# Float32 score matmuls in place of three float32r passes in the second attention step

## The chip, the core and the metric

The kernel runs on one core of one Trainium2 chip. TensorE (PE in the profile, with its weight loads as PEld) multiplies matrices, VectorE (DVE) and ScalarE (ACT) work element by element, GpSimd (POOL) does a few element-wise operations beside them, and SyncE (SP) issues most of the DMAs. The metric is the device time of one execution in microseconds (us), the median of several runs.

## What is computed

The reference is a two-step attention followed by two feed-forward layers:

```python
def sm_attn(qq, kk, vv):
    s = scale * np.matmul(qq, kk.transpose(0, 1, 3, 2))
    s = s - np.max(s, axis=-1, keepdims=True)
    a = np.exp(s)
    a = a / (np.sum(a, axis=-1, keepdims=True) + 1e-09)
    return np.matmul(a, vv)
p_packed = sm_attn(p, k, v)            # 32 packs attend to 576 tokens
out = sm_attn(q, p_packed, p_packed)   # 576 tokens attend to 32 packs
...
x = out.transpose(0, 2, 1, 3).reshape(4608, 512)
h = x @ w_in;  x = (h * np.cos(h)) @ w_out                 # first layer, d_ff 2048
h = x @ w_in2; x = (P(h) / (Q(h) + 1e-6)) @ w_out2         # second layer, d_ff 2048
```

There are 8 batches of 8 heads, 576 tokens, a head dimension of 64 and 32 packs. All values are float32. The change is in the scores of the second `sm_attn`: queries against packed rows.

## The kernel before, in words

The work is cut into groups of one batch and four heads, 16 groups in all (two per batch, `g` = 0 and 1). Most matmuls run on float32r operands: a float32 value `x` is carried as `hi + lo`, and a product takes the three passes of `PASSES` (hi·hi, hi·lo, lo·hi). `split` (lines 65 to 67) makes such a pair: ACT copies the value into `hi` (L66) and another engine subtracts to get `lo` (L67).

The kernel has four stretches.

1. *Pack attention* (to about 204 us in the profile). For each group `prep` transposes k on DVE into `kT` (L177) and lays p out block-diagonally on POOL (`pbd`, L182). `s1` takes the scores of packs against tokens with float32 operands (four matmuls, L209), then come the softmax (L217 to L228), the transposes `et` (L238), the product with v (`pv`, L249), and `wunit` (L283), which multiplies the packed rows with the first layer's input weights. Beside this, `conv_w1i` turns these weights from float64 words into float32r pairs: `convert` (lines 74 to 93) is four instructions on DVE (L82, L87, L89, L90), three on ACT (L80, L88, L92) and two on POOL (L91, L93) for each 128x512 block.
2. *Conversion of the first layer's output weights* (`conv_w1o`, some 204 to 281 us), in which the first slots of the next stretch already run.
3. *First layer* (about 281 to 930 us). There are 128 slots, each with 12 matmuls for `h` (`mm_h`, L530), an element-wise chain on ACT and DVE (`chain1`, L554 to L561, then `finish_g`, which splits `g` into `gh` and `gl`), and 24 matmuls for `y` two slots later (`mm_y`, L574). `h` has two PSUM buffers: PE can start the `h` of a slot only when the last DVE instruction that reads the one before last (L561) is done. `split_wq` (four blocks for each batch, ACT L66 and POOL L67) and `conv_w2` (one block in three slots) run beside it.
4. *Second layer* (from 930 us), with no POOL work at all.

The second attention step is `attn2_steps`, a generator that is advanced between other work: for batch 0 inside stretch 1, for batches 1 to 7 inside stretches 2 and 3, one step every second slot. For one group it loads q and the packed rows, transposes both on DVE (`qT` L327, `ppT` L333), and **splits both**: ACT writes `qh` and `pph`, POOL subtracts to get `ql` and `ppl`, through L66 and L67. One step later come twelve float32r matmuls (`scores`, L193) into a PSUM buffer that it shares with `h` (tag "h") or, in stretch 1, with `s1`. DVE transposes the scores out (`sT`, L343) and the softmax follows.

The instructions of an engine run in the order in which they stand in its queue. That order is set by a scheduler that works on the program as a whole; `hold` keeps some instructions behind a given matmul. In stretch 1 `qT` shares its two buffers with `kT`, and `ppT` with `pbd` (the table `tg0`).

## Time and profile before

| what | value |
|---|---|
| runs | 1743.73, 1744.01, 1751.22 us; median 1744.01 us |
| span of the profiled execution | 1744.9 us |
| PE busy | 1619.0 us, 93% of the span |
| DVE busy | 1424.5 us, 82% |
| ACT busy | 1175.8 us, 67% |
| POOL busy | 355.0 us, 20% |
| mean granted TensorE clock | 0.973 of full |

Busy time of an engine is the time in which at least one of its instructions ran. A matmul's record is longer than the distance to the next one, since matmuls are pipelined; the distance between starts tells what a matmul costs in a stream. A float32 matmul of the program shows as two records. The span differs from the median of the runs by 0.9 us; no other time of the profiled execution is listed.

### The profile page before, as it was taken

Reading aid. Unit: us, or ns where it says so; the run is one execution under the profiler, and the core shown is the slowest. Engines: PE = TensorE matmul, PEld = TensorE weight load, DVE = VectorE, ACT = ScalarE, POOL = GpSimd, SP = SyncE. Lnnn points to the kernel's source line nnn. Section 1 sums busy time; section 2 is a strip of 40 time slices with the busy share of each in tenths; the row PEclk is TensorE's granted clock in tenths of the full one; section 3 lists DMA queues with packets and bytes.
Section 4 is the critical chain, followed back from the end, with each engine's and each line's share of the span. In section 5 each row is a group of like instructions: output and inputs, shape, how many; then the busy total and the mean of one; then the engine's idle time right before and its main releaser. Section 6 shows DMA issues by size and latency. Waiting matters only on the chain.

```text
span 1744.9 us, 24418 instructions
## 1 busy us (share of the span) xinstructions
PE 1619.0 (93%) x8896; PEld 1419.4 (81%) x8896; DVE 1424.5 (82%) x2143; ACT 1175.8 (67%) x1917; POOL 355.0 (20%) x235
## 2 busy tenths in 40 slices
PE   5889578999899989899999999999999999999996
PEld 3668378989899989889898888888888888888884
DVE  6993598798889889988867888888888888888884
ACT  4554566666656566666547787878787878787874
POOL 4650553434334434343300000000000000000000
PEclk9989789999999999999999999999999999999998
DMA  9897822443434434433348020202020202020000
GB/s 291 249 258 234 271 88 83 135 134 113 141 120 134 135 122 136 140 129 107 130 161 304 1 72 1 72 1 73 1 73 1 73 0 72 2 72 1 31 19 25
DMA packets 99768, 183.52 MB, mean 105 GB/s; under 512 B 11584, under 2 KB 46400, under 8 KB 99648
## 3 DMA queue, kind: packets, MB, share of 16 engines
q1 hardware_dynamic: 92224, 163.09, 29.3%
q10 hardware_dynamic: 7424, 18.88, 3.5%
q8 instruction: 70, 1.15, 0.3%
q14 instruction: 50, 0.41, 0.1%
HBM read 117.97 MB, written 63.96 MB: 104 GB/s over the span
## 4 chain that ended last, share of the span: by engine, by line
PE 66%; DVE 20%; ACT 5%; issue 4%; DMA 3%; POOL 1%; SPq 0%; ACTq 0%; DVEq 0%
PE h L659 23%; PE o L718 23%; PE y L574 11%; PE h L530 6%; DVE gl L67 3%; DVE u L555 3%; DVE cvp L89 2%; DVE r L556 2%; DVE cvp L87 2%; DVE g L561 2%; DVE cvf L90 1%; DVE cvf L82 1%; DMA st<-in_moe_w_in_dram 1%; PE w L283 1%; PE s L209 1%
## 5 line engine op out<-in xcount | busy, mean ns | idle before, releaser
L574 PE MATMUL y<-gh,w1o 128*128 128x288 f32 x2048 | 431.8, 297 | 2.3 <-DVE yl L67 2.3
L659 PE MATMUL h<-x,w 128*128 128x512 f32 x1728 | 422.7, 393 | 0.0
L659 PEld LDWEIGHTS h<-x,w 128*128 128x128 f32 x1728 | 324.1, 188 | 74.2
L574 PEld LDWEIGHTS y<-gh,w1o 128*128 128x128 f32 x2048 | 338.1, 190 | 3.8 <-DVE yl L67 3.2
L718 PE MATMUL o<-w,g2h 128*128 128x512 f32 x1152 | 334.0, 394 | 1.3 <-ACT g2h L677 1.3
L574 PE MATMUL y<-gl,w1o 128*128 128x288 f32 x1024 | 298.7, 297 | 15.0 <-DVE gl L67 14.7
L530 PE MATMUL h<-ah,wq 128*128 128x288 f32 x1024 | 236.2, 307 | 46.0 <-DVE g L561 43.2
L718 PEld LDWEIGHTS o<-w,g2h 128*128 128x128 f32 x1152 | 216.0, 188 | 53.1 <-ACT g2h L677 2.1
L530 PEld LDWEIGHTS h<-ah,wq 128*128 128x128 f32 x1024 | 179.5, 197 | 51.0 <-issue 49.4
L574 PEld LDWEIGHTS y<-gl,w1o 128*128 128x128 f32 x1024 | 193.3, 189 | 18.9 <-DVE gl L67 18.9
L718 PE MATMUL o<-w,g2l 128*128 128x512 f32 x576 | 199.9, 393 | 0.0
L693 ACT ACTIVATE sq<-h 128x512 f32<-128x512 f32 x144 | 87.4, 607 | 155.7 <-PE h L659 155.6
L560 ACT ACTIVATE r<-r,coef 128x576 f32<-128x576 f32 x128 | 99.1, 775 | 103.1 <-DVE r L556 102.4
L695 DVE SCALAR_TENSOR_TENSOR ab<-sq,coef,ab 128x512 f32<-128x512 f32 x144 | 108.1, 751 | 67.8 <-ACT ab L694 67.5
L530 PE MATMUL h<-al,wq 128*128 128x288 f32 x512 | 156.1, 305 | 0.0
L67 DVE TENSOR_TENSOR gl<-g,gh 128x576 fp32r<-128x576 f32 x128 | 126.3, 989 | 18.0 <-ACT gh L66 16.3
L704 DVE SCALAR_TENSOR_TENSOR ab<-ab,y 128x512 f32<-128x512 f32 x144 | 99.5, 691 | 48.1 <-ACT y L701 47.5
L91 POOL TENSOR_TENSOR cvf<-cvf,cvs 128x512 f32<-128x512 f32 x64 | 88.2, 1377 | 217.7 <-DVE cvf L90 216.5
L554 ACT ACTIVATE u<-h,coef 128x576 f32<-128x576 f32 x128 | 93.8, 734 | 54.3 <-PE h L530 53.8
L718 PEld LDWEIGHTS o<-w,g2l 128*128 128x128 f32 x576 | 108.0, 188 | 25.6
L696 ACT ACTIVATE c<-h,coef 128x512 f32<-128x512 f32 x144 | 114.1, 792 | 9.8 <-DVE g2l L683 9.8
L561 DVE TENSOR_TENSOR g<-h,r 128x576 f32<-128x576 f32 x128 | 95.9, 750 | 30.1 <-ACT r L560 29.9
(97 smaller groups left out, 2775.6 us busy)
## 6 DMA issues: line engine op xcount, KB each, us to landing
x<-yd SPq DMA_DIRECT2D x36, 512.0 KB
w<-w2d SPq DMA_DIRECT2D x68, 256.0 KB
st<-in_moe_w_in_dram SPq DMA_DIRECT2D x32, 512.0 KB
wd<-wev ACTq DMA_DIRECT2D x64, 256.0 KB
st<-in_moe_w_out_dram SPq DMA_DIRECT2D x32, 512.0 KB
wq<-wd SPq DMA_DIRECT2D x32, 512.0 KB
kx<-in_k_dram SPq DMA_DIRECT2D x16, 576.0 KB
vx<-in_v_dram SPq DMA_DIRECT2D x48, 192.0 KB
```

What stands on the lines that cost most here:

```text
L67: lo_eng.tensor_tensor(out=lo, in0=src, in1=hi.bitcast(F32), op=ALU.subtract)
L91: nc.gpsimd.tensor_tensor(out=ff, in0=ff, in1=sg, op=ALU.mult)
L530: last_h[0] = nc.tensor.matmul(out=ps[:, u, 0:HS], lhsT=wq[:, g, a, o:o + 128], rhs=a_t[b, g][c][:, hf * HS:hf * HS + HS], start=(i == 0), ...
L554: nc.scalar.activation(out=u, in_=ph, func=AF.Identity, scale=INV2PI, bias=coef[:, 6:7])
L560: nc.scalar.activation(out=r, in_=r, func=AF.Sin, bias=coef[:, 7:8])
L561: nc.vector.tensor_tensor(out=gt, in0=ph, in1=r, op=ALU.mult)
L574: nc.tensor.matmul(out=y_t[d][:, 0:HS], lhsT=w1o_s[f // 4][a][:, f % 4, 128 * d:128 * d + 128], rhs=gs[c][:, u], start=(f == 0 and i == 0) ...
L659: nc.tensor.matmul(out=ps, lhsT=w2_s[f][:, 0, a, 128 * kk:128 * kk + 128], rhs=x_t[t, c, kk], start=(i == 0), stop=(i == 3 * NKD - 1),)
L695: nc.vector.scalar_tensor_tensor(out=ab, in0=sq, scalar=coef[:, 5:6], in1=ab, op0=ALU.mult, op1=ALU.add)
L696: nc.scalar.activation(out=c1, in_=ph, func=AF.Identity, scale=coef[:, 3:4], bias=coef[:, 2:3])
L704: nc.vector.scalar_tensor_tensor(out=ab, in0=ab, scalar=QC, in1=y0, op0=ALU.add, op1=ALU.mult)
L718: nc.tensor.matmul(out=o_t[s], lhsT=g2_t[n][a][:, 128 * s:128 * s + 128], rhs=w2_s[f][:, 1, c], start=(f == 0 and i == 0), stop=(f == NFC ...
```

## The change

`scores` now takes one float32 operand on each side and makes four matmuls for a group (two halves of the tokens, two blocks of the head dimension) where it made twelve. `s1`, which had the same loop written out, calls it. In `attn2_steps` both splits are gone, with their four tiles and with their instructions on ACT and POOL; the matmuls read `qT` and `ppT` themselves.

```diff
-        def scores(ps, lhs, rhs, lhs_of):
-            for hf in range(2):
-                i = 0
-                for e in range(NDB):
-                    for a, c in PASSES:
-                        nc.tensor.matmul(
-                            out=ps[:, hf, 0:HS],
-                            lhsT=lhs_of(lhs[a], e),
-                            rhs=rhs[c][:, e, hf * HS:hf * HS + HS],
-                            start=(i == 0),
-                            stop=(i == 3 * NDB - 1),
-                        )
-                        i += 1
...
+        def scores(ps, lhs, rhs):
             for hf in range(2):
                 for e in range(NDB):
                     nc.tensor.matmul(
                         out=ps[:, hf, 0:HS],
-                        lhsT=pbd[:, e],
-                        rhs=kT[:, e, hf * HS:hf * HS + HS],
+                        lhsT=lhs[:, e],
+                        rhs=rhs[:, e, hf * HS:hf * HS + HS],
                         start=(e == 0),
                         stop=(e == NDB - 1),
                     )
...
-                qs = [tile([128, NDB, S], F32R, nm) for nm in ("qh", "ql")]
-                split(*qs, qT.rearrange("p e c j -> p e (c j)"), nc.gpsimd)
-                ps = [tile([128, NDB, 4 * M], F32R, nm) for nm in ("pph", "ppl")]
-                split(*ps, ppT.rearrange("p e h m -> p e (h m)"), nc.gpsimd)
...
-                scores(sc, ps, qs, lambda x, e: x[:, e])
+                scores(sc, ppT.rearrange("p e h m -> p e (h m)"), qT.rearrange("p e c j -> p e (c j)"))
```

Line numbers after the change are smaller by 12 from L217 to L333 and by 16 from L343 on; `s1`'s matmuls, L209 before, are L191 now, and so are those of the second step.

On POOL, in the conversion of the first layer's output weights (`cvf` and `w1o` are its blocks), the difference between the two orders is this:

```order
 L93 TENSOR_TENSOR w1o<-cvf,w1o 128x512
 L91 TENSOR_TENSOR cvf<-cvf,cvs 128x512
-L67 TENSOR_TENSOR ql<-qT,qh 128x1152
-L67 TENSOR_TENSOR ppl<-ppT,pph 128x256
 L93 TENSOR_TENSOR w1o<-cvf,w1o 128x512
 L91 TENSOR_TENSOR cvf<-cvf,cvs 128x512
```

The two subtractions are gone and their neighbours stand as they stood. The same holds for the other 15 pairs but for a few neighbours that change places.

On DVE, in the middle of the first layer (the step of batch 4 that begins with `qT`; `cvf` and `cvp` belong to a block of `conv_w2`, `yl` to the split of `y`, `gl`, `u`, `r` to the element-wise chain), the rows before are:

```order
L82 TENSOR_SCALAR cvf<-st_5045 128x512
L327 STREAM_TRANSPOSE qT<-qx 128x18x2x32
L333 STREAM_TRANSPOSE ppT<-ppx 128x4x2x32
L87 TENSOR_SCALAR cvp<-cvf 128x512
L67 TENSOR_TENSOR yl<-y_4569,yh 128x288
L67 TENSOR_TENSOR gl<-g,gh 128x576
L555 TENSOR_SCALAR u<-u 128x576
L67 TENSOR_TENSOR yl<-y_4570,yh 128x288
L89 TENSOR_TENSOR cvp<-st_5045,cvp 128x512
```

and now:

```order
L82 TENSOR_SCALAR cvf<-st_4917 128x512
L315 STREAM_TRANSPOSE qT<-qx 128x18x2x32
L321 STREAM_TRANSPOSE ppT<-ppx 128x4x2x32
L87 TENSOR_SCALAR cvp<-cvf 128x512
L67 TENSOR_TENSOR yl<-y_4441,yh 128x288
L67 TENSOR_TENSOR gl<-g,gh 128x576
L539 TENSOR_SCALAR u<-u 128x576
L67 TENSOR_TENSOR yl<-y_4442,yh 128x288
L89 TENSOR_TENSOR cvp<-st_4917,cvp 128x512
```

Nothing moved at this place on DVE.

On DVE, in the pack attention, around the first scores of batch 0 (`kT` is the next groups' k for `s1`, `sT` takes the scores out of PSUM; in brackets the engines and DMA queues waited for), the rows before are:

```order
L177 STREAM_TRANSPOSE kT<-kx 128x3x6x32 [waits DMAHW2_49,Pool_49]
L177 STREAM_TRANSPOSE kT<-kx 128x3x6x32
L67 TENSOR_TENSOR wl_328<-pt,wl_327 128x64 [waits Activation_49]
L217 TENSOR_REDUCE mx<-s_545 128x1 [waits PE_49]
L177 STREAM_TRANSPOSE kT<-kx 128x3x6x32 [waits DMAHW2_49]
L177 STREAM_TRANSPOSE kT<-kx 128x3x6x32
L82 TENSOR_SCALAR cvf<-st_311 128x512 [waits DMAHW3_49,Pool_49]
```

and now, where the second pair is further down:

```order
L205 TENSOR_REDUCE mx<-s_537 128x1 [waits PE_49]
L177 STREAM_TRANSPOSE kT<-kx 128x3x6x32 [waits DMAHW2_49]
L177 STREAM_TRANSPOSE kT<-kx 128x3x6x32
L87 TENSOR_SCALAR cvp<-cvf 128x512 [waits DVE_49]
...
L67 TENSOR_TENSOR wl_328<-pt,wl_327 128x64 [waits Activation_49]
L327 STREAM_TRANSPOSE sT<-s_629 128x576 [waits PE_49]
L177 STREAM_TRANSPOSE kT<-kx 128x3x6x32 x2
L90 SCALAR_TENSOR_TENSOR cvf<-cvp,cvf 128x512 [waits DVE_49,Activation_49]
```

A pair of k's transposes that took over the buffer of `qT` waited for POOL's subtraction; it now stands behind the transpose of the scores, since the buffer is free only when the score matmuls have read it.

## Rows read from the trace of the kernel before

**Rows 1.** Stretches: us, busy us of each engine (instructions), granted clock, DMA share, GB/s

```profile
36.00:123.00 87.00, 67.97 (x289) 52.42 (x287) 84.18 (x142) 47.63 (x95) 51.70 (x40) 0.86 0.90 253
204.00:281.00 77.00, 52.15 (x340) 50.36 (x340) 71.38 (x91) 45.07 (x71) 42.14 (x29) 0.84 0.35 111
281.00:930.00 649.00, 610.34 (x4444) 601.05 (x4445) 548.08 (x773) 398.87 (x600) 224.30 (x129) 0.98 0.41 134
930.00:1744.90 814.90, 798.75 (x3455) 647.04 (x3453) 662.62 (x1012) 630.06 (x1047) 0.00 (x0) 0.99 0.13 42
```

**Rows 2.** Groups of instructions: count, busy us, mean ns, idle before

```profile
L67 POOL TENSOR_TENSOR ql<-qT,qh 128x1152 fp32r<-128x1152 f32 x16 | 44.3, 2771 | 41.6 <-ACT qh L66 41.6
L66 ACT ACTIVATE qh<-qT 128x1152 fp32r<-128x1152 f32 x16 | 18.7, 1168 | 10.0 <-DVE qT L327 10.0
```

**Rows 3.** Timeline from 499.8 us: start, us, instruction, idle before it

```profile
500.02 2.98 POOL L67 TENSOR_TENSOR ql<-qT,qh 128x1152 fp32r<-128x1152 f32 x1 [7.42 <-ACT qh L66]
500.73 2.81 DVE L89 TENSOR_TENSOR cvp<-st,cvp 128x512 f32<-128x512 uint32 x1
...
506.65 0.58 PE L530 MATMUL h<-ah,wq 128*128 128x288 f32 x1 [2.40 <-DVE g L561]
```

**Rows 4.** DVE instructions by tile: duration ns, min/median/max

```profile
L555 DVE TENSOR_SCALAR u<-u x128: 396/454/2918, 215.3 to 919.9; 128x576 f32<-128x576 f32 x128
L87 DVE TENSOR_SCALAR cvp<-cvf x64: 382/427/2627, 16.4 to 836.4; 128x512 uint32<-128x512 uint32 x64
L89 DVE TENSOR_TENSOR cvp<-st,cvp x64: 643/692/2902, 17.6 to 840.6; 128x512 f32<-128x512 uint32 x64
L90 DVE SCALAR_TENSOR_TENSOR cvf<-cvp,cvf x64: 641/682/3111, 19.3 to 841.6; 128x512 f32<-128x512 f32 x64
```

**Rows 5.** Chain that ended last: start, us, what

```profile
43.03 2.37 DVE cvp L87
...
67.73 3.03 DVE cvf L90
...
231.97 2.84 DVE u L555
```

**Rows 6.** Timeline from 259.5 us, DVE

```profile
260.35 3.09 DVE L90 SCALAR_TENSOR_TENSOR cvf<-cvp,cvf 128x512 f32<-128x512 f32 x1
```

**Rows 7.** Twelve stretches of 8 us, each from a start of `ql` after 281

```profile
500.00:508.00 8.00, 5.60 (x39) 5.40 (x38) 7.83 (x11) 4.30 (x8) 5.58 (x4) 0.89 0.59 206
...
615.40:623.40 8.00, 4.84 (x26) 4.64 (x25) 7.25 (x11) 4.65 (x9) 3.54 (x2) 0.72 0.41 152
...
769.80:777.80 8.00, 5.59 (x38) 5.38 (x38) 7.83 (x11) 4.29 (x8) 5.58 (x4) 0.88 0.58 200
...
sum 96.00, PE 82.89 PEld 80.72 DVE 90.39 ACT 57.48 POOL 53.29; mean PE 6.91 PEld 6.73 DVE 7.53 ACT 4.79 POOL 4.44
```

**Rows 8.** Float32 matmuls of `s1`, by tile: duration ns, min/median/max

```profile
L209 PE MATMUL s<-kT,pbd x128: 403/406/847, 9.0 to 159.1; 128*128 128x288 f32 x128
```

**Rows 9.** Chain, the same matmuls of two groups

```profile
107.13 3.62 PE s L209 x8
...
133.05 1.94 PE s L209 x8
```

**Rows 10.** Timeline of PE: first score matmul of a group, first matmul behind it

```profile
248.01 0.29 PE L193 MATMUL s<-qh,pph 128*128 128x288 f32 x1
...
249.60 0.30 PE L574 MATMUL y<-gh,w1o 128*128 128x288 f32 x1
```

**Rows 11.** The other splits on POOL, grouped

```profile
L67 POOL TENSOR_TENSOR wq<-wq 128x1024 fp32r<-128x1024 f32 x32 | 79.3, 2482 | 121.2 <-ACT wq L66 121.0 <-PE h L530 0.2
L67 POOL TENSOR_TENSOR al<-aT,ah 128x576 fp32r<-128x576 f32 x16 | 26.9, 1684 | 24.1 <-ACT ah L66 24.1
```

**Rows 12.** Transposes on DVE in the pack attention and of the scores, grouped

```profile
L177 DVE STREAM_TRANSPOSE kT<-kx 128x576 f32<-128x576 f32 x32 | 23.0, 752 | 8.7 <-DMA kx<-in_k_dram 8.7
L343 DVE STREAM_TRANSPOSE sT<-s 128x576 f32<-128x576 f32 x16 | 12.4, 777 | 6.2 <-PE s L193 6.2
```

More of the change, by code (lines that the diff above doesn't have):

```diff
@@ L186, in prep @@
             pbd_t[n] = pbd.rearrange("p e h m -> p e (h m)")
-        def scores(ps, lhs, rhs, lhs_of):
-            for hf in range(2):
-                i = 0
-                for e in range(NDB):
-                    for a, c in PASSES:
-                        nc.tensor.matmul(
-                            out=ps[:, hf, 0:HS],
-                            lhsT=lhs_of(lhs[a], e),
-                            rhs=rhs[c][:, e, hf * HS:hf * HS + HS],
-                            start=(i == 0),
-                            stop=(i == 3 * NDB - 1),
-                        )
-                        i += 1
-        E_t, rd_t = {}, {}
-        def s1(n):
-            ps = ps0.tile([128, 2, 512], F32, tag="s1", name="s1")
-            pbd, kT = pbd_t.pop(n), kT_t.pop(n)
+        def scores(ps, lhs, rhs):
             for hf in range(2):
@@ L215, in s1 @@
                     )
+        E_t, rd_t = {}, {}
+        def s1(n):
+            ps = ps0.tile([128, 2, 512], F32, tag="s1", name="s1")
+            scores(ps, pbd_t.pop(n), kT_t.pop(n))
             mx = wk.tile([128, 1], F32, tag="mx", bufs=2, name="mx")
```

## The prediction

> **What bounds the kernel now.** I read the stretches first [rows 1], since the shares over the whole run mix four limits. From 930 us on PE is busy for 798.8 of 814.9 us and POOL does nothing: the second layer is bound by PE, and no part of the change reaches it. In the first layer, 281 to 930 us, PE is busy for 610.3 of 649.0 us. It sets the pace there, yet 38.7 us of idle time are left to win. DVE is busy for 548.1 us of it, so PE's idle time has to come from places where DVE falls behind for a moment. Before that it is the other way round: from 36 to 123 us DVE is busy for 84.2 of 87 us and from 204 to 281 us for 71.4 of 77. There DVE sets the pace, and what it saves is saved on the path.
>
> Then I looked at what the removed work does to the others. The larger of a group's two splits, that of q, is in the groups [rows 2]: 1.17 us on ACT and 2.77 us on POOL, 16 times each; the split of the packed rows, less than a quarter as wide, stands beside it. Neither engine is a bound, so by busy time alone they would be worth nothing. The timeline shows otherwise [rows 3]: POOL's `ql` runs from 500.02 for 2.98 us, a DVE instruction that starts in it (L89) takes 2.81 us and ends 0.54 us after it, and PE then stands idle for 2.40 us until DVE's L561 has freed a buffer of `h`. The same L89 takes 0.69 us as a rule [rows 4]. So a subtraction on POOL holds some of DVE's instructions for as long as it runs. The four DVE forms of [rows 4] have medians of 0.43 to 0.69 us and longest cases of 2.6 to 3.1 us, about the length of `ql`. The chain of waits passes through such cases: L87 at 43.03, L90 at 67.73, L555 at 231.97 [rows 5]; a fourth is L90 at 260.35 [rows 6].
>
> **The change, part by part.**
>
> *Twelve float32r matmuls become four float32 ones.* The first of twelve starts at 248.01 and the next matmul behind them at 249.60 [rows 10]: 1.59 us a group, 0.1325 each. What four float32 matmuls of the same 288 columns cost is shown by `s1`: they are eight records [rows 8], and the chain gives them 1.94 us at 133.05 [rows 9]. So PE pays 0.35 us more for a group. Twelve of the 16 groups lie after 281 us, where PE sets the pace: +4.2 us. The other four lie where DVE does; their 1.4 us are hidden behind its work and would be added if that cover went. The nearest other row is the piece at 107.13, 3.62 us, in a stretch whose mean granted clock is 0.86 [rows 1, 9]: at that price twelve groups would cost 24 us more. I take 0.35, since the granted clock is 0.98 where the twelve stand. A gain is excluded: PE runs the eight records in one stream, with its weight loads beside them.
>
> The Trainium skill, "FP8 and Floating Point Precision", section "TensorE Precision Notes", says that true float32 takes four passes through the array. Four passes at the float32r spacing of [rows 10] would be 16 times 0.1325, or 2.12 us, against the 1.94 that the trace shows: +6.4 us instead of +4.2, and a forecast of 1730 instead of 1728. The row decides.
>
> *POOL's subtractions go, first layer.* After 281 us there are twelve. The 8 us from the start of each one, taken together, hold 82.9 us of PE work in 96 [rows 7]: 13.1 of the 38.7 us of idle time lie in 15% of the time. Where a stall was long, the granted clock fell too: its mean is 0.89, 0.72 and 0.88 in the stretches from 500.0, 615.4 and 769.8 [rows 7]. The clock has two levels, 1.2 and 2.4 GHz, so a mean of 0.89 over 8 us is 0.9 us of lost work, and the three make 0.9 + 2.2 + 1.0 = 4.1 us. All of it, 17.2 us, is the upper bound. The lower one is nothing: the stalls come back elsewhere (first rival). I take 10 of 13.1 and 4 of 4.1: DVE stands in the same order there with or without the splits, so the L89 of [rows 3] will be 2.1 us shorter with nothing else put in its place; but the transposes `qT` and `ppT` stay on DVE ahead of the slot's chain, and I can't tie every microsecond of the idle time to `ql`. +14 us saved. What is late next at these places is L561 still, only by less.
>
> *The same, conversion stretch.* Two subtractions, at the two DVE cases of 2.84 and 3.09 us [rows 5, 6]. Less their medians, 0.45 and 0.68 [rows 4], that is 4.8 us of a DVE that is busy for 93% of the stretch. I take 4.5; nothing if ACT or POOL turn out late instead, 4.8 if all is kept.
>
> *The same, pack attention.* Two subtractions, 2.37 - 0.43 and 3.03 - 0.68 [rows 4, 5]: 4.3 us of DVE. Against this stands a new wait. A pair of k's transposes for `s1` goes into the buffer that `qT` had and must now wait for the score matmuls on PE; it stands behind the transpose of the scores, with L90 of a weight block queued behind it, and `s1`, its reduction and its softmax wait for it. The DMA queues, too, are at 0.90 there [rows 1]. I take 2 of the 4.3; the ends are 4.3 saved and, if the new wait is bare, a loss (last rival).
>
> *ACT's copies go.* For q alone 14 times 1.17 us [rows 2] from 204 us on, 16 us, on an engine busy for 399 of 649 us [rows 1]. I count nothing: ACT's work is hidden behind PE, and where it delays the chain of a slot (qh stands ahead of a `u`), the idle time of [rows 7] holds it already.
>
> *Sum.* 14 + 4.5 + 2 - 4.2 = 16.3 us less. The profiled execution's span is 1744.9 us, 0.9 above the median of 1744.0; span less sum is 1728.6, and the median that follows is 1727.7, so **1728 us**. The best case by the bounds is 17.2 + 4.8 + 4.3 - 4.2 = 22.1, or 1722, and some 6 us more if the clock also stays up in the DVE-bound stretches, where 16% of 77 us and 14% of 87 us are lost to it [rows 1] and a part follows these stalls: an estimate of 1716.
>
> **The rivals.**
>
> *The stalls move.* 32 subtractions of `wq` and 16 of `al` stay, of 2.48 and 1.68 us [rows 11], beside those of the conversions. A DVE instruction that no longer waits for `ql` comes 2 us sooner and may meet one of these. For it: the 25.6 us of idle time outside [rows 7] are of the same kind, so any shift throws the dice again. Against it: DVE's total work falls, and PE's need rises only 0.35 us a group. If the whole gain of the first layer is lost in this way, 4.5 + 2 - 4.2 is left: 1742 us, no change to be told.
>
> The Trainium skill gives the mechanism, "SBUF — State Buffer", section "Who interferes with whom": VectorE in its two-port modes or with two SBUF inputs and GpSimd share a port pair as an exclusive lock, and whichever issues first holds it for its whole instruction. The trace agrees for the length [rows 3, 4]. By that rule order alone decides, which is what this rival needs.
>
> *The new wait in the pack attention decides.* Twice (two groups of batch 0) `s1` of the next group waits for score matmuls, their transpose and two transposes of k. Bare, that is a chain of 1.94 us of scores [rows 9], 0.78 of transpose and twice 0.75 of k's transposes [rows 12], 4.2 us, and as much again when the softmax behind it starts late: 8 us a place, 16 in all. With the 4.2 of PE and the first rival's loss of the gain, but the conversion stretch's 4.5 kept, this gives 1744.0 + 16 + 4.2 - 4.5 = 1760 us, slower. It decides from the point where DVE has no other instruction ready during the wait. Against it: DVE is 97% busy there with conversion work that doesn't need k.
>
> *The float32 passes are dearer in the first layer than in `s1`.* At 3.62 us a group the loss is 24 instead of 4.2, and with all gains kept the time is 1747. For it: only the piece at 107.13. Against it: the eight records of 403 to 406 ns, the rule in this trace [rows 8].
>
> **How the numbers follow.** The forecast's case has a chance of 0.70, with its own range of 1716 to 1735; the stalls move, 0.20; the new wait, 0.06; dearer passes, 0.04. A measurement of this kernel tells about 0.5%, 8.7 us, from no change: faster is under 1735.3 and slower above 1752.7. The forecast's case gives 0.70 of faster and the second one some 0.02; same has 0.18 of it and the 0.04 of dear passes; slower has the 0.06. I put 0.72, 0.21 and 0.07. The range is 1715 to 1745: the low end is the best case, the high end takes in the second case.
>
> **What would show it.** Right: the longest cases of L555, L87, L89 and L90 (L555 is L539 now) still reach 2.4 us, but only beside `wq`, `al` and the conversions; PE's busy time in the first layer is at least 4 us more while the stretch is some 10 us shorter; the eight records of a group's scores take 1.9 us. Wrong: PE's idle time between the conversion's end and the second layer stays at 38 us or more; or the stretch to 123 us is longer than before, with DVE idle ahead of a transpose of k. The forecast would be wrong altogether if DVE's long cases stayed as many as they are: then POOL's `ql` was not what held them.

## The result, and the profile after

The changed kernel took 1714.41 us in the median (1713.67 to 1715.93) beside 1743.87 us for the kernel before (1743.03 to 1751.22): a ratio of 0.9823, 95% interval 0.9802 to 0.9844. Measured once more in a later job it was 1709.94 against 1747.16 us, 0.9786 (0.9770 to 0.9801). The forecast was 1728, with a range of 1715 to 1745: the direction was right, and the gain is 29 to 37 us, not 16.

The profiled execution of the changed kernel has a span of 1711.9 us, against 1744.9. Its stretches, cut as in [rows 1] (us, busy us and instructions of PE, PEld, DVE, ACT and POOL, granted clock, DMA share, GB/s):

```profile
36.00:123.00 87.00, 71.13 (x298) 55.01 (x298) 78.50 (x147) 46.60 (x94) 47.84 (x38) 0.89 0.91 263
204.00:277.00 73.00, 54.31 (x342) 52.19 (x341) 67.85 (x92) 42.58 (x68) 35.49 (x25) 0.84 0.37 115
277.00:897.00 620.00, 603.41 (x4388) 591.66 (x4387) 518.42 (x772) 383.54 (x573) 181.47 (x105) 0.99 0.43 140
897.00:1711.90 814.90, 798.71 (x3454) 647.01 (x3453) 662.54 (x1012) 629.63 (x1047) 0.00 (x0) 0.99 0.13 42
```

The second layer takes 814.9 us as before. In the first, 620.0 us against 649.0, PE's idle time is 16.6 us against 38.7, which is 22.1 of the 29.0 us. The other 6.9 are PE's own busy time, 603.4 us against 610.3, although the float32 matmuls are dearer: the granted clock is 0.99 against 0.98.

The twelve stretches of [rows 7], now from 3 us after the start of each `qT` transpose (`ql` used to start 2.6 to 3.9 us after it):

```profile
491.60:499.60 8.00, 7.67 (x58) 7.47 (x57) 7.38 (x12) 4.36 (x8) 2.58 (x2) 1.00 0.83 276
...
597.10:605.10 8.00, 8.00 (x62) 8.00 (x62) 6.06 (x11) 5.09 (x9) 2.00 (x2) 1.00 0.38 138
...
744.10:752.10 8.00, 7.63 (x58) 7.42 (x57) 7.38 (x13) 4.37 (x7) 2.59 (x2) 1.00 0.83 272
...
sum 96.00, PE 95.31 PEld 94.60 DVE 84.01 ACT 58.49 POOL 18.19; mean PE 7.94 PEld 7.88 DVE 7.00 ACT 4.87 POOL 1.52
```

PE works for 95.3 of 96 us where it worked for 82.9, and the granted clock is 1.00 in all twelve, also where it was 0.89, 0.72 and 0.88. The L89 that took 2.81 us in [rows 3] is at the same place again, and is short:

```profile
488.56 1.37 DVE L315 STREAM_TRANSPOSE qT<-qx 128x1152 f32<-128x1152 f32 x1
...
492.30 0.68 DVE L89 TENSOR_TENSOR cvp<-st,cvp 128x512 f32<-128x512 uint32 x1
```

The four DVE forms of [rows 4] (ns, min/median/max; L555 is L539 now):

```profile
L539 DVE TENSOR_SCALAR u<-u x128: 397/455/2686, 214.0 to 886.8; 128x576 f32<-128x576 f32 x128
L87 DVE TENSOR_SCALAR cvp<-cvf x64: 378/428/2509, 18.6 to 807.8; 128x512 uint32<-128x512 uint32 x64
L89 DVE TENSOR_TENSOR cvp<-st,cvp x64: 643/689/1930, 19.8 to 810.4; 128x512 f32<-128x512 uint32 x64
L90 DVE SCALAR_TENSOR_TENSOR cvf<-cvp,cvf x64: 622/684/1755, 21.5 to 811.6; 128x512 f32<-128x512 f32 x64
```

Long cases remain, but none of 2.8 to 3.1 us is left, and each of the five DVE instructions that exceed the median of their kind by over 2 us runs beside a `wq` subtraction. The float32 records of the scores are those of `s1` [rows 8], and a group of them stands in PE's stream like this:

```profile
L191 PE MATMUL s<-qT,ppT x128: 404/406/687, 54.9 to 781.0; 128*128 128x288 f32 x128
```

```profile
505.72 2.10 PE L191 MATMUL s<-qT,ppT 128*128 128x288 f32 x8
507.45 0.51 PE L514 MATMUL h<-ah,wq 128*128 128x288 f32 x1
507.80 0.30 PE L514 MATMUL h<-al,wq 128*128 128x288 f32 x1
```

The group takes 1.73 us up to the next matmul, and that one holds the stream for 0.35 us where 0.13 is usual: 1.95 us, against the 1.94 of the forecast.

For the experiments I cut the span at three matmul starts that every kernel has: the first `h`, the `h` of slot 16 (second batch), and the second layer's first. The last part is 819.6 or 819.7 us in all of them. Each stretch is read from one profiled execution; the two of the changed kernel differ by 3.7, 0.9 and 2.0 us, so less than that tells nothing.

| us | pack attention | conversion, first batch | rest of first layer |
|---|---|---|---|
| before | 205.2 | 104.7 | 615.4 |
| changed | 204.6 | 100.7 | 586.9 |
| changed, later job | 200.9 | 99.8 | 584.9 |

### The profile page after: what moved, and what is told of

It is laid out like the page before. It is cut to its first block, busy times and chain, and to the rows that moved or that the text cites. A ratio compares the mean times of both kernels' runs of the same rounds, so it can differ in the third digit from the quotient of the medians.

```text
span 1711.9 us, 24200 instructions
## 1 busy us (share of the span) xinstructions
PE 1614.5 (94%) x8832; PEld 1412.0 (82%) x8832; DVE 1382.4 (81%) x2143; ACT 1155.9 (68%) x1885; POOL 298.0 (17%) x203
## 4 chain that ended last, share of the span: by engine, by line
PE 74%; DVE 15%; ACT 4%; issue 3%; DMA 3%; SPq 0%; POOL 0%; ACTq 0%; DVEq 0%; POOLq 0%
PE h L643 23%; PE o L702 23%; PE y L558 14%; PE h L514 7%; PE s L191 3%; DVE gl L67 2%; DVE u L539 2%; DVE g L545 2%; DVE cvp L87 2%; PE w L271 1%; DVE cvp L89 1%; DVE r L540 1%; PE pv L237 1%; DVE cvf L90 1%; DMA st<-in_moe_w_in_dram 1%
## 5 line engine op out<-in xcount | busy, mean ns | idle before, releaser
L514 PE MATMUL h<-ah,wq 128*128 128x288 f32 x1024 | 232.2, 303 | 26.9 <-DVE g L545 24.9
L514 PEld LDWEIGHTS h<-ah,wq 128*128 128x128 f32 x1024 | 175.2, 192 | 30.4 <-issue 27.4
L67 DVE TENSOR_TENSOR gl<-g,gh 128x576 fp32r<-128x576 f32 x128 | 117.1, 917 | 18.2 <-ACT gh L66 16.1
L702 PEld LDWEIGHTS o<-w,g2l 128*128 128x128 f32 x576 | 108.0, 188 | 25.6
```

Source lines behind the costliest of these rows:

```text
L67: lo_eng.tensor_tensor(out=lo, in0=src, in1=hi.bitcast(F32), op=ALU.subtract)
L514: last_h[0] = nc.tensor.matmul(out=ps[:, u, 0:HS], lhsT=wq[:, g, a, o:o + 128], rhs=a_t[b, g][c][:, hf * HS:hf * HS + HS], start=(i == 0), ...
L702: nc.tensor.matmul(out=o_t[s], lhsT=g2_t[n][a][:, 128 * s:128 * s + 128], rhs=w2_s[f][:, 1, c], start=(f == 0 and i == 0), stop=(f == NFC ...
```

## Experiments

Every ratio is to the kernel before, run on the same chip in the same job; the stretches are those of the table.

**Putting parts back.** In the first the changed kernel gets POOL's two subtractions as unused work:

```diff
+                nc.gpsimd.tensor_tensor(out=jq, in0=qv, in1=qv, op=ALU.subtract)
+                nc.gpsimd.tensor_tensor(out=jp, in0=pv_, in1=pv_, op=ALU.subtract)
```

> The changed kernel with POOL's two subtractions of each group put back as work whose result nobody reads (128x1152 and 128x256 float32, from qT and from ppT); ACT's copies stay out and the scores stay float32. The instructions of DVE, ACT and PE stand nearly in the order of the changed kernel. Theory POOL (the subtractions hold DVE and PE then waits; all of the gain is theirs): about 1744 + 5 for the dearer scores, 1742 to 1752 us, with PE idle for some 40 us in the first layer. Theory ACT (the two copies in ACT's queue delayed the chain of a slot): 1714 to 1718. Theory order (another order of the program happens to put fewer DVE instructions beside the subtractions that stay): about 1720, since the order is the new one, plus at most the 14 us that the prediction gave to the places of ql.

Measured: 1.0004 (0.9992 to 1.0015); pack 212.2, conversion 103.2, rest of the first layer 610.2 us. POOL's work alone takes the whole gain back. From slot 16 on this kernel runs in the changed kernel's order: the instructions that both have follow one another alike on PE, DVE and POOL, and on ACT in all but 6 of 1580 places. PE's idle time there is 32.3 us, less than the 40 that were expected. The unused subtraction of q reads one tile twice and takes 2.11 us in the median, where the real one took 2.70, so it stands for a little less work than was removed. Then ACT's copies alone:

```diff
+                nc.scalar.activation(out=jq, in_=qv, func=AF.Copy)
+                nc.scalar.activation(out=jp, in_=pv_, func=AF.Copy)
```

> The changed kernel with ACT's two copies of each group put back (results unused), nothing on POOL. Theory POOL: 1713 to 1720 us, since POOL stays free. Theory ACT: 1730 to 1745, with the idle time of PE in the first layer back to 30 us or more. Theory order: between 1714 and 1744, as the order falls out, with the long DVE instructions beside wq, al and the conversions making the difference.

Measured: 0.9952 (0.9937 to 0.9967); 214.1, 103.3 and 599.1 us. So ACT's copies, which the forecast counted at nothing, seemed to cost over 20 us, with 23.8 us of idle time of PE in the last stretch and not the 30 of the ACT theory. Both splits, unused:

```diff
+                split(*qs, qv, nc.gpsimd)
+                split(*ps, pv_, nc.gpsimd)
```

> The changed kernel with both splits computed in full and unused; only the matmuls are the new ones. What is left of the change is the price of float32 on PE and the freedom of the matmuls from waiting for the splits. Theory POOL and theory ACT alike: 1746 to 1752 us, before plus 4 to 6. Theory order: 1720 to 1750, and not tied to the splits.

Measured: 1.0065 (1.0048 to 1.0082); 214.1, 109.0 and 618.3 us, in an execution 5 us above the median. The median, 1758.2 us, lies 6 us above what any of the theories had. From slot 16 on the order is nearly the second experiment's (38 of DVE's 1748 places differ), so POOL's splits cost 19 us there. And from the other side, the kernel before without POOL's subtractions:

```diff
-                split(*qs, qT.rearrange("p e c j -> p e (c j)"), nc.gpsimd)
+                nc.scalar.activation(out=qs[0], in_=qT.rearrange("p e c j -> p e (c j)"), func=AF.Copy)
...
-                split(*ps, ppT.rearrange("p e h m -> p e (h m)"), nc.gpsimd)
+                nc.scalar.activation(out=ps[0], in_=ppT.rearrange("p e h m -> p e (h m)"), func=AF.Copy)
```

> The kernel before with its twelve float32r matmuls a group and ACT's copies, but without POOL's two subtractions: the matmuls take the hi parts in all three passes, so the low parts are left out of the scores. DVE and PE stand nearly in the order of the kernel before. Theory POOL: 1744 less 34, about 1708 to 1714 us, below the changed kernel because the matmuls are the cheaper ones. Theory ACT: 1738 to 1744. Theory order: 1727 to 1735, the 14 us at the places of ql and no more, since the order is the old one.

Measured: 0.9936 (0.9920 to 0.9951); 210.9, 99.7 and 601.8 us. This is what the theory of order had (0.9936 of 1744 is 1733 us). POOL's work is worth 13.6 us of the first layer here, and 23 when put into the changed kernel. The parts don't add up, so something else moves with them.

**The yardstick, and the length of one POOL instruction.** The changed kernel, unaltered:

> The changed kernel itself, unaltered, as the yardstick for the other kernels timed beside it and for the four earlier experiments, in which the kernel before stood at 1748.42 us. Steady-chip theory: the ratio repeats, 0.982 of the kernel before within 0.003, with the start of the first `h` matmuls at 205 us as in its first profile, so that the 211 to 214 us of the four earlier experiments belong to those kernels. Chip theory: the start of the first `h` matmuls moves to 211 us or later here too, and then the packing stretch says nothing on the change.

Measured: the 0.9786 above, just under the 0.979 that was expected, with a pack stretch of 200.9 us where 205 was. The four kernels above ran on another chip than this one, so this alone doesn't show that their 211 to 214 us belong to them; for the order of the second one it is shown below, where that order has 214.5 us on this chip. Next the subtraction of q in four pieces:

```diff
+                for e in range(NDB):
+                    for x in range(2):
+                        c = slice(x * HS, x * HS + HS)
+                        nc.gpsimd.tensor_tensor(out=jq[:, e, c], in0=qv[:, e, c], in1=qv[:, e, c], op=ALU.subtract)
+                nc.gpsimd.tensor_tensor(out=jp, in0=pv_, in1=pv_, op=ALU.subtract)
```

> The changed kernel with the low-part subtraction of q put back on POOL as unused work, but in four pieces of 288 columns instead of one of 1152 (in the earlier experiment the one piece took 2.11 us in the median and the kernel came to 1.000 of the kernel before). Theory that the length of one POOL instruction does it (VectorE can get in between two pieces, and an early piece's wait is short enough for the slack): 0.982 to 0.986 of the kernel before, stretched VectorE instructions at these places of at most about 0.7 us, no idle time of TensorE over 1 us at them. Rival, that POOL's total time against VectorE counts: within 0.003 of 1.000, as with one piece. Rival, that only POOL's work between other POOL work (the splits of wq and of the conversions pushed late) counts: also near 1.000, with the long idle times of TensorE at the wq splits and not at the q pieces.

Measured: 0.9943 (0.9925 to 0.9962); 206.0, 108.1 and 601.0 us: between the changed kernel and the one with a single piece. A place in its timeline:

```profile
413.42 3.27 POOL L328 TENSOR_TENSOR ql<-qT 128x288 f32<-128x288 f32 x4 [2.16 <-DVE qT L315]
413.59 0.81 DVE L547 TENSOR_SCALAR u<-u 128x576 f32<-128x576 f32 x1
...
415.60 0.40 PE L566 MATMUL y<-gl,w1o 128*128 128x288 f32 x1 [0.89 <-DVE gl L67]
```

DVE's `u` waits for one piece only, and PE stands for 0.89 us. But the four pieces take POOL 3.27 us, so more DVE instructions meet one: 31 are at least 0.25 us longer than the median of their kind, by 12.8 us in all, against 16 and 26.6 us with one piece. PE's waits behind the pieces (slots 3, 4 and 8 of a batch) are 0.3 to 1.4 us, where the theory of length had at most 1. The order hardly differs: from slot 16 on, all but 32 of DVE's 1748 places are as in the changed kernel. Length counts, and it is not all. ACT's copies with 16 columns each, against the second experiment:

```diff
-                nc.scalar.activation(out=jq, in_=qv, func=AF.Copy)
-                nc.scalar.activation(out=jp, in_=pv_, func=AF.Copy)
+                nc.scalar.activation(out=jq[:, 0, 0:16], in_=qv[:, 0, 0:16], func=AF.Copy)
+                nc.scalar.activation(out=jp[:, 0, 0:16], in_=pv_[:, 0, 0:16], func=AF.Copy)
```

> The changed kernel with ScalarE's two copies put back as unused work, but of 16 columns each instead of 1152 and 256 (full copies: 0.9952 of the kernel before, against 0.982 without). They still stand in ScalarE's queue behind the transposes of q and p, and wait for them. Theory that ScalarE's 1.58 us at each of 16 places counts (what stands behind the copies starts so much later, and the written order shifts with them): 0.982 to 0.986. Rival, that the wait for VectorE's transposes at the head of ScalarE's queue counts (up to 1.9 us idle there in the full version): stays at 0.993 to 0.997. By either theory the pieces of POOL are those of the changed kernel.

Measured: 0.9839 (0.9824 to 0.9854); 209.5, 100.8 and 586.6 us. I read it as ACT's time, too early. From slot 16 on, this kernel runs PE, DVE and ACT in the changed kernel's order to the last instruction, where with full copies 149 of DVE's 1749 places hold another one. So it can't tell ACT's time from the order.

**Order and work apart.** The next kernels hold every engine and queue to a written order taken from another build, by edges that only set who stands behind whom:

```diff
+        row = [per[e][n + dl[n]] for n in range(m)]
+        for x, y in zip(row, row[1:]):
+            tc.add_manual_dep(
+                y, x.name, mybir.DependencyInfo(mybir.DependencyClass.NoSync, mybir.DependencyReason.SCHED_ONLY),
+                reason="issue order",
+            )
```

`row` is one engine's instructions, `dl` a table of how far each moves. First the changed kernel in the order of the kernel with the copies, without the copies:

> The changed kernel with not one instruction more or less, but with every engine and queue held to the written order that the builder gave the kernel with ScalarE's two copies put back (537 of VectorE's 2143 instructions and 1967 of TensorE's stand elsewhere than in the changed kernel; the copies themselves are absent). Theory that ScalarE's removed copies gained by the time that they took in ScalarE's queue: the changed kernel's 0.979 to 0.983 of the kernel before, its 585 to 587 us from slot 16 of the first layer to the second layer and its batches of 84 to 85 us. Rival, that the copies' removal gained by what it did to the written order: what the kernel with the copies had, 0.993 to 0.997, some 599 us, batches of 87 to 88 us.

Measured: 0.9956 (0.9940 to 0.9971); 214.5, 103.1 and 598.4 us. Then the copies, in the changed kernel's order:

```diff
+                extra.append(nc.scalar.activation(out=jq, in_=qv, func=AF.Copy))
+                extra.append(nc.scalar.activation(out=jp, in_=pv_, func=AF.Copy))
```

> The changed kernel in its own written order on every engine and queue, with ScalarE's two copies of q and p put in as unused work (1.17 and 0.40 us, 16 times). Theory that their time in ScalarE's queue counts: 0.990 to 0.997 of the kernel before, 595 to 600 us from slot 16 of the first layer to the second layer, new idle times of TensorE a slot or two behind the copies. Rival, that the written order counts: the changed kernel's 0.979 to 0.983 and 585 to 588 us. Half of either: both, at 592 us.

Measured: 0.9809 (0.9792 to 0.9827); 201.9, 100.5 and 584.5 us. The rest of the first layer, the order alone first, the copies second:

```profile
317.60:916.00 598.40, 573.04 (x4154) 561.70 (x4154) 503.48 (x738) 361.68 (x544) 170.49 (x101) 0.99 0.42 139
```

```profile
302.40:887.00 584.60, 567.81 (x4155) 556.87 (x4154) 494.88 (x738) 379.47 (x569) 172.60 (x101) 1.00 0.43 142
```

With 16 us more on ACT the stretch is as short as without; in the other order, without the copies, it is 12 to 14 us longer than the changed kernel's 586.9 and 584.9 with the same work. The theory that ACT's time counts has fallen. One of the places where the orders differ, ACT in the third batch, the order with the copies first, with PE's wait behind it (start, us, instruction, idle before it):

```profile
458.19 0.74 ACT L539 ACTIVATE u<-h,coef 128x576 f32<-128x576 f32 x1 [2.02 <-PE h L515]
...
460.77 1.17 ACT L338 ACTIVATE sT<-sT 128x1152 f32<-128x1152 f32 x1
461.84 0.72 ACT L539 ACTIVATE u<-h,coef 128x576 f32<-128x576 f32 x1
462.58 1.28 ACT L545 ACT_TABLE_LOAD   x1
463.88 0.78 ACT L545 ACTIVATE r<-r,coef 128x576 f32<-128x576 f32 x1
...
465.59 0.37 PE L515 MATMUL h<-ah,wq 128*128 128x288 f32 x1 [1.07 <-DVE g L546]
```

and the changed kernel:

```profile
445.62 0.74 ACT L538 ACTIVATE u<-h,coef 128x576 f32<-128x576 f32 x1
446.38 1.28 ACT L337 ACT_TABLE_LOAD   x1
447.67 1.17 ACT L337 ACTIVATE sT<-sT 128x1152 f32<-128x1152 f32 x1
448.86 1.28 ACT L544 ACT_TABLE_LOAD   x1
450.15 0.78 ACT L544 ACTIVATE r<-r,coef 128x576 f32<-128x576 f32 x1
450.83 0.72 ACT L538 ACTIVATE u<-h,coef 128x576 f32<-128x576 f32 x1
```

With the copies' order the next slot's `u` stands ahead of `r`, so `r` comes later; DVE's `g` waits for `r`, and the next `h` matmul for `g`. Last of this group, POOL's work in the changed kernel's order:

```diff
+                extra.append(nc.gpsimd.tensor_tensor(out=jq, in0=qv, in1=qv, op=ALU.subtract))
+                extra.append(nc.gpsimd.tensor_tensor(out=jp, in0=pv_, in1=pv_, op=ALU.subtract))
```

> The changed kernel in its own written order on every engine and queue, with POOL's two subtractions put in as unused work (2.1 and 0.4 us, 16 times). Theory that they hold VectorE at their own places: nearly all of what they cost with the order free, 0.996 to 1.001 of the kernel before, 606 to 611 us from slot 16 to the second layer, with idle times of TensorE of 1.7 to 2.6 us in slots 3 and 8 of the batches. Rival, that most of their cost was the written order: at most a third of the 24 us between 610 and 586, under 594 us.

Measured: 0.9982 (0.9971 to 0.9994); 207.4, 104.0 and 609.8 us. POOL's work costs 23 to 25 us in the first layer by itself, the order untouched. A place:

```profile
414.49 2.11 POOL L326 TENSOR_TENSOR ql<-qT 128x1152 f32<-128x1152 f32 x1 [2.16 <-DVE qT L316]
...
414.66 2.25 DVE L545 TENSOR_SCALAR u<-u 128x576 f32<-128x576 f32 x1
...
418.05 0.40 PE L564 MATMUL y<-gl,w1o 128*128 128x288 f32 x1 [2.27 <-DVE gl L68]
```

**The change itself, cut into order and work.** From the first `h` on, the changed kernel is held to the order of the kernel before:

```diff
+    for i in list(nc.cur_bb.bb.instructions)[start:]:
```

> The changed kernel's instructions, from the first `h` matmul on held on every engine and queue to the written order of the kernel before (the packing stretch keeps whatever order the builder gives). Theory that half of the gain in the first layer is the written order: 597 to 603 us from slot 16 of the first layer to the second layer, as with POOL's subtractions taken out of the kernel before (601.8), where the changed kernel has 585 to 587; about 0.990 to 0.996 of the kernel before. Rival, that the changed instructions alone bring it: 585 to 590 us.

Measured: 0.9874 (0.9859 to 0.9888), rest of the first layer 600.6 us. The kernel before in the changed kernel's order, where its own splits stand free:

```diff
+                extra.update(i.name for i in list(nc.cur_bb.bb.instructions)[n0:])
```

> The kernel before's instructions (both splits, three passes) held on every engine and queue to the written order of the changed kernel, the three passes where the float32 matmuls stood. Theory that POOL's subtractions decide there: 604 to 610 us from slot 16 to the second layer, as with them alone in that order (609.8 us), less 4 for the passes, and 0.994 to 1.000 of the kernel before. Rival, that the order alone brings most of the gain: under 594 us and under 0.988.

Measured: 0.9967 (0.9954 to 0.9980); 206.5, 104.2 and 607.1 us. The twelve stretches of 8 us of these two, the changed work in the old order first:

```profile
sum 96.00, PE 95.17 PEld 94.53 DVE 86.77 ACT 57.91 POOL 19.90; mean PE 7.93 PEld 7.88 DVE 7.23 ACT 4.83 POOL 1.66
```

```profile
sum 96.00, PE 82.23 PEld 80.07 DVE 91.15 ACT 56.42 POOL 52.88; mean PE 6.85 PEld 6.67 DVE 7.60 ACT 4.70 POOL 4.41
```

At these places the work decides alone: 95.2 and 95.3 us of PE without `ql` in either order, 82.2 and 82.9 with it. What the order gives lies elsewhere. The rest of the first layer of the kernel before, of the changed work in the old order, and of the old work in the new order (the changed kernel's row stands further down):

```profile
309.90:925.20 615.30, 576.66 (x4201) 567.97 (x4201) 525.21 (x736) 376.06 (x567) 215.80 (x125) 0.98 0.41 134
301.80:902.30 600.50, 576.15 (x4153) 564.33 (x4153) 506.67 (x736) 359.93 (x543) 171.19 (x101) 0.99 0.42 138
310.70:917.80 607.10, 575.92 (x4202) 568.63 (x4201) 513.09 (x738) 377.99 (x569) 218.11 (x125) 0.98 0.42 136
```

From the old order to the new one, with the changed work, PE's idle time falls from 24.4 to 16.1 us and its busy time from 576.2 to 570.8 us for the same matmuls. The clock makes most of the second part: PE was busy for 16.3 us at the lower of its two levels, 1.2 GHz, in the old order, and for 6.8 us in the new one (21.7 in the kernel before, 23.4 with the old work in the new order). This split is less firm than the sum: the fourth experiment, nearly in the old order, has 33.6 us of idle time and 568.2 of busy time, and about the same length. Part of the idle time that went lies in slot 14 of the batches, at the subtractions of `wq`, where five idle times of 11.1 us in sum became four of 7.0. In two of these batches POOL's order differs; one of them, in the old order and then in the changed kernel, with PE's wait behind it:

```profile
545.34 2.82 POOL L68 TENSOR_TENSOR wq<-wq 128x1024 fp32r<-128x1024 f32 x1 [16.41 <-ACT wq L67]
548.11 1.87 POOL L68 TENSOR_TENSOR al<-aT,ah 128x576 fp32r<-128x576 f32 x1
549.94 1.49 POOL L92 TENSOR_TENSOR cvf<-cvf,cvs 128x512 f32<-128x512 f32 x1
551.97 0.37 PE L515 MATMUL h<-ah,wq 128*128 128x288 f32 x1 [2.77 <-DVE g L546]
```

```profile
543.23 1.84 POOL L67 TENSOR_TENSOR al<-aT,ah 128x576 fp32r<-128x576 f32 x1 [14.98 <-ACT ah L66]
545.04 2.85 POOL L67 TENSOR_TENSOR wq<-wq 128x1024 fp32r<-128x1024 f32 x1
548.52 1.42 POOL L91 TENSOR_TENSOR cvf<-cvf,cvs 128x512 f32<-128x512 f32 x1 [0.63 <-DVE cvf L90]
549.62 0.37 PE L514 MATMUL h<-ah,wq 128*128 128x288 f32 x1 [1.71 <-DVE g L545]
```

The same as the last kernel, but without POOL's subtractions (edit as in the fourth experiment):

> The kernel before without POOL's subtractions (the low parts of q and p left out, the high parts in all three passes), with ScalarE's copies, held to the written order of the changed kernel. Theory that order and POOL together make the whole gain, and that ScalarE's copies and the passes' form hardly count: 580 to 587 us from slot 16 to the second layer and 0.976 to 0.982, where the same instructions in their own order had 601.8 us and 0.9936. Rival, that float32 scores are what gains: 596 us or more.

Measured: 0.9766 (0.9749 to 0.9782); 207.9, 99.8 and 585.8 us, in an execution 8 us above the median of its five. With ACT's copies and three float32r passes it is as fast as the changed kernel:

```profile
307.70:893.60 585.90, 567.42 (x4203) 561.09 (x4202) 495.20 (x738) 378.52 (x570) 173.28 (x101) 0.99 0.43 141
```

The changed kernel's row for this stretch:

```profile
305.30:892.20 586.90, 570.84 (x4154) 559.93 (x4153) 493.07 (x738) 363.45 (x545) 172.93 (x101) 0.99 0.44 141
```

PE is busy for 3.4 us less with the passes at the same granted clock, and the stretch is 1.0 us shorter. That is less than the 2.0 us between the two profiles of the changed kernel, so how much of the float32 price reaches the time isn't told.

The rest of the first layer, us, by the order from slot 16 on and by POOL's two subtractions:

| order | with them | without them |
|---|---|---|
| of the kernel before | 615.4 | 600.6; 601.8 (fourth experiment) |
| of the changed kernel | 607.1; 609.8 and 610.2 as unused work | 586.9 and 584.9; with ACT's copies 584.5 and 585.8 |

The fourth experiment's order is that of the kernel before in all but 20 of DVE's 1748 places.

The last test moved two pairs of ACT's 1885 instructions; its table differs from the changed kernel's in four entries, two neighbours swapped in each of two batches:

> The changed kernel in its own written order, but for two of ScalarE's instructions: in the third and the sixth batch the softmax exponential (1.17 us, with a table load of 1.28 us on either side) stands ahead of the `u` of slot 10 or 11 instead of behind it, as in the order with the copies. Theory that this place makes part of the order's cost: an idle time of TensorE of 1 to 1.6 us in slot 12 of these two batches, which are 1.5 to 4 us longer, and 2 to 7 us in all. Rival, that TensorE has the slack for it: within 1.5 us of the changed kernel's 585 to 587 us from slot 16 to the second layer.

Measured: 0.9813 (0.9795 to 0.9830), within the spread of the changed kernel's two ratios; rest of the first layer 590.6 us, 4 to 6 more. The edit missed its target: it hit the second and the fifth batch, and it is not quite the move that the other order makes. In the second batch, where the changed kernel's PE has no wait for this `h`:

```profile
359.17 1.17 ACT L339 ACTIVATE sT<-sT 128x1152 f32<-128x1152 f32 x1 [0.90 <-DVE sT L335]
...
360.24 0.73 ACT L540 ACTIVATE u<-h,coef 128x576 f32<-128x576 f32 x1
...
365.06 0.37 PE L516 MATMUL h<-ah,wq 128*128 128x288 f32 x1 [1.25 <-DVE sm L342]
```

In the fifth batch a wait grows from 1.6 to 2.5 us. So two neighbours swapped suffice for about 1 us of idle time of PE, 2.1 us for both pairs; how much of the 14 us this kind of place makes isn't shown.

**A faster version.** The subtraction for `wq` in quarters:

```diff
+            for g in range(G):
+                for x in (slice(0, 256), slice(256, 512)):
+                    eng.tensor_tensor(
+                        out=t[:, g, 1, x], in0=t[:, g, 1, x].bitcast(F32), in1=t[:, g, 0, x].bitcast(F32),
+                        op=ALU.subtract,
+                    )
```

> The changed kernel with the subtraction that splits wq on POOL (32 of them, one instruction of 1024 columns, 2.4 us) cut into four of 256 columns; nothing else. Theory that a long POOL instruction holds VectorE: 22.5 us of VectorE's stretched time in the first layer lie under these 2.4 us instructions, and 14 of the 18.3 us of idle time of TensorE over 0.3 us lie at them with two stretches of low clock of 3.4 us; most of it goes: 1700 to 1708 us beside 1714 for the changed kernel, a ratio of 0.975 to 0.979. Rival, that those idle times come from the order of the work around wq: the changed kernel's time within 3 us, 0.982. Rival, that four instructions cost POOL more than they spare (each has its fixed part, and a wq that is split later holds the `h` matmuls): slower than the changed kernel, above 0.984.

Measured: 1703.28 us, 0.9744 (0.9728 to 0.9761), against 0.9786 for the changed kernel in the same job; rest of the first layer 580.5 us. It beats both kernels. Its `wq` group and its `u` on DVE:

```profile
L443 POOL TENSOR_TENSOR wq<-wq 128x256 fp32r<-128x256 f32 x128 | 106.0, 861 | 99.1 <-ACT wq L440 99.1
```

```profile
L545 DVE TENSOR_SCALAR u<-u x128: 395/458/1591, 212.7 to 876.7; 128x576 f32<-128x576 f32 x128
```

POOL pays 106.0 us for what cost 80.5 in the changed kernel, and the longest `u` falls from 2.69 to 1.59 us. The order isn't what gained here: PE and DVE run in the changed kernel's order throughout, ACT in all but 12 of 1868 places. With `al` in halves as well:

```diff
+                for x in (slice(0, HS), slice(HS, S)):
+                    nc.gpsimd.tensor_tensor(out=al[:, x], in0=av[:, x], in1=ah[:, x].bitcast(F32), op=ALU.subtract)
```

> The changed kernel with POOL's subtractions of wq in quarters, as in the experiment that came to 0.9744, and those of al in halves of 288 columns as well. Theory that the remaining long POOL instructions still hold VectorE: 7.5 us of stretched VectorE time lie under al, of which half goes, and some of it is on the path: 0.971 to 0.974, 576 to 580 us from slot 16 to the second layer (580.5 with wq in quarters alone). Rival, that al's places have slack: 0.974 to 0.976, 580 to 582 us.

Measured: 0.9771 (0.9755 to 0.9787), rest of the first layer 582.4 us: nothing gained over 580.5, near what the rival had. That the places of `al` have slack fits this and was not tested further.

## Why the prediction was right in direction and wrong in size

- *POOL's subtractions, first layer: 14 us, at most 17.2.* Right in its cause, too small in size. PE's work in the twelve stretches rose by 12.4 us (82.89 to 95.31), nearly all of the 13.1. The 4.1 us of clock were misread: they count all of the 8.0 us at the lower level, and PE was busy in 6.0 of them, some 3.0 us of work. The changed work in the old order measures 615.4 - 600.6 = 14.8 us net of the dearer matmuls, where the step less 4.2 gave 9.8 and its upper bound 13.0; outside the twelve places, too, idle time fell by 2.0 us with the work alone.
- **The step that failed** is the sum, 14 + 4.5 + 2 - 4.2. Its 14 rest on the sentence "DVE stands in the same order there with or without the splits, so the L89 of [rows 3] will be 2.1 us shorter with nothing else put in its place". At that place it held. But it was carried over to the whole stretch: the sum has no term for the order that the scheduler writes anew when 64 instructions go and 192 matmuls become 64, and so leaves the 25.6 us of idle time outside [rows 7], and the clock there, as they were. From slot 16 on, 237 of DVE's 1749 places hold another instruction than before. With the changed work, that term is 600.6 - 586.9 = 13.7 us (15.7 against the later job's 584.9): 8.3 us of PE's idle time and 5.3 of its busy time, at a higher granted clock. The spans differ by 33.0 us where 16.3 were forecast, and the 16.7 that are missing are this stretch: it gave 28.5 us instead of 9.8, and the two stretches ahead of it 1.9 less than forecast.
- *The stalls move (the first rival).* It named the right thing, the order of what lies outside [rows 7], but priced it only as a loss. The 25.6 us of idle time there became 16.6 - 0.7 = 15.9. By the rule of the Trainium skill that the rival cited ("SBUF — State Buffer", "Who interferes with whom") order decides who is held; the traces agree so far as the same work left PE idle for 24.4 us in one order and 16.1 in another, and no run here says beforehand in which direction a new order goes. That it went the good way was not foreseen: the right direction of the forecast rests on POOL's work, and half of the gain on the order.
- *ACT's copies: nothing.* Right, 584.5 against 584.9 us with them in the same order. What the second experiment lost was the order that they bring.
- *Float32 matmuls: +4.2 us.* The group takes 1.95 us, as forecast, and PE's busy time shows 3.4 at an equal clock. The sign that PE would be busy for 4 us more in the first layer did not come (603.4 us against 610.3), since the clock gave back more than that.
- *Conversion stretch: 4.5 us.* 104.7 to 100.7 or 99.8: right.
- *Pack attention: 2 us.* 0.6 in the first profile, 4.3 in the second, so the size isn't told. The new wait did not show in the time. The order weighs more here: 201.9 us in the changed kernel's order with ACT's copies, 214.5 in the other without them.
- Order and work don't add: the order alone gives 615.4 - 607.1 = 8.3 us, the work alone 14.8, both 28.5 to 30.5. PE's idle time nearly adds: 7.5 us less by the order, 14.3 by the work, 22.6 by both. Its busy time does not: 0.7 and 0.5 us less by either, 5.8 by both. So in these profiles most of what the parts lack is in the granted clock: 0.98 with the order alone, 0.99 with the work alone, 0.99 or 1.00 with both. Which differences of the order make the 14 us is shown for single places only; the rest is open.

## What to carry to other kernels

Where a scheduler writes the order, removing an instruction is two changes: the instruction, and the order of all others; price the first from the trace and widen the range by what the order alone can do (here 14 to 16 us in the first layer and 10 to 14 in the pack attention). To tell them apart, pin the order of one build onto the work of the other before blaming an engine's busy time. A long GpSimd instruction beside a busy VectorE is worth cutting into pieces where VectorE is on the path, as with `wq` here; with `al` it gained nothing.

## What the runs showed of the hardware

- One unused subtraction of 1152 columns took POOL 2.11 us in the changed kernel, four of 288 columns 3.27 us at the place shown: the pieces cost it half as much again, and the rest of the first layer was still 9 us shorter with them (601.0 against 610.2, both nearly in the changed kernel's order there).
- PE's work at the places of `ql` was the same in two quite different orders (82.2 and 82.9 us in 96): a hold of 2 to 3 us on VectorE was not absorbed by a better order.
- The same matmuls kept PE busy for 576.2 us in one order and for 570.8 and 567.8 in two runs of another. PE was busy at 1.2 GHz for 16.3, 6.8 and 0 us of it. The idle time does not foretell this: the fourth experiment had 33.6 us of idle time and 3.4 us at that level, the changed work in the old order 24.4 and 16.3.
